# First pair's loads split over two queues, its bounds over three banks, its masks turned in two parts, and a new instruction order, in a chunk-selecting attention kernel on one core

## The chip, the core and the metric

The kernel runs on one core of one Trainium2 chip. The metric is the device time of one execution in microseconds (us); the median of the runs stands for a kernel. PE is the matrix engine (PEld its weight loads), DVE the vector engine, ACT the scalar engine, POOL the general one, SP the one that issues most DMAs. Each runs its instructions strictly in the order written, and waits on semaphores for the others.

## The reference

Attention over selected chunks of keys, then a gated linear unit with a causal convolution, in float32; four batches, eight heads, 768 positions, head size 64.

```python
k_chunks = k.reshape(B, H, nc, chunk, D)            # chunk = 32, nc = 24
k_min, k_max = np.min(k_chunks, axis=3), np.max(k_chunks, axis=3)
ub = np.sum(np.maximum(q[:, :, :, None, :] * k_min[:, :, None, :, :],
                       q[:, :, :, None, :] * k_max[:, :, None, :, :]), axis=-1)
ub = np.where(causal, ub, -1000000000.0)
top_chunks = np.argsort(ub, axis=-1)[..., -top_k:]  # top_k = 6
scores = scale * np.matmul(q, k.transpose(0, 1, 3, 2))
scores = np.where(mask, scores, -1000000000.0)      # selected chunk, and causal
attn = softmax(scores)
x = concatenate_heads(np.matmul(attn, v))           # (4, 768, 512)
gate = 1.0 / (1.0 + np.exp(-gate_pre))              # gate_pre: causal convolution of x, 5 taps
out = (gate * (x @ w_val)) @ w_out
```

## The kernel before

Two heads make a pair; there are 16 pairs (0 to 15), four to a batch, and each has six query tiles of 128 positions (0 to 5). A function `build` makes a graph of named operations, and `emit_in_order` writes them down in the order of a long table, `ORDER`. That table alone sets the order on each engine; `=7` behind a name is the PSUM bank (of eight) that the operation's group takes. A bank is free again when the last operation of its group has been written. No scheduler runs later.

The names, for pair p: `Lk`, `Lq`, `Lv` load keys, queries, values (for pair 0 keys and queries in two halves of 384 positions, `.0` and `.1`, each as two DMAs, one for each head, 96 KB apiece). `KT`, `QT` transpose them on PE (half `.0` or `.1`), `KE`, `QH` copy the result on ACT. `KX` reduces a half to the maximum or the minimum of each chunk on DVE. Only pair 0 computes its bounds in float32: `KF` copies the maxima (`.h0`) and the minima with the sign turned (`.h1`) of head h, `QF` and `RF` are the two parts of the queries by sign, on ACT, and `BF0.t` is the product for query tile t, one matmul with the causal fill and four passes of the float32 ones. (Later pairs do it with `QL`, `AH`, `AL` on DVE, `KB` on POOL and `CF`, `BD` on PE.) `T8` takes the eight largest bounds of a tile and head, `CM` compares with the sixth, which gives the mask `NS`. `MT` turns the masks of five tiles on PE, `ME` copies them to `QM` on DVE; `MD` does both as a DMA for pairs 10 to 15. `Sp.b` is a bank of scores (two matmul groups, one with the mask), `E` the exponential on ACT, `A` the causal cut on POOL, `AV` the product with the values (`VC` made them on POOL), `RC` and `NR` the division on DVE. `XT` turns the result, by DMA on SP for pairs 8 to 14, by PE and a copy `XTE` otherwise. `XH` copies the halo on POOL, `CV` is the convolution on PE, `TH` the gate on ACT, `VL` and `GV` the value product and the gating, `OU`, `OE`, `ST` the last product, its eviction and its store. `F0` to `F15` and `G0` to `G19` are filler matmuls on zeros that keep PE busy; `cwt` and `cws` turn the convolution's weights; `aw` is a small exponential that nothing reads.

Loads, stores and DMA transposes stand in one queue on SP, in the table's order. A DMA also waits until the one eight places earlier has landed, since eight semaphores are used in turn. Pair 0's five bound products share one bank, so `T8`, which waits for its bank, begins after the last of them.

## Time and profile before

| | us |
|---|---|
| runs of the kernel before (3) | 187.21 median, 186.26 to 188.31 |
| the profiled execution | 186.9 |
| its span in the profile | 185.2 |

A row of the timeline has start and length in us, engine, line of the code, operation, what it writes and reads, how many were merged, and in brackets the idle time before it with what ended it. A row of a stage table has the stretch and each engine's busy time in it. Busy time of PE counts matmuls from their start to their end, with their latency, so that PE can be busy and still have room. The granted clock was 1.00 throughout.

### The profile page before, as it was taken

The numbers are of one execution on the slowest core, as the hardware profiler recorded it, in microseconds if no ns is written. First come the engines' busy times: TensorE is split into PE (matmuls) and PEld (weight loads), VectorE is DVE, ScalarE is ACT, GpSimd is POOL, SyncE is SP. The second block draws the span as 40 slices with busy tenths as digits, with TensorE's granted clock in tenths as the row PEclk, the third lists the DMA queues.
The fourth block names the chain that finished last, engine by engine and source line by source line (L and its number), as shares of the span: only waits on it lengthen the run. The fifth ranks groups of instructions, "written<-read, shape, count | busy, mean of one in ns | idle before, by whom it ended". The sixth has DMA issues, their size and how long they took to land.

```text
span 185.2 us, 8893 instructions
## 1 busy us (share of the span) xinstructions
PE 176.5 (95%) x3714; PEld 127.2 (69%) x3714; DVE 125.8 (68%) x429; ACT 140.3 (76%) x320; POOL 109.6 (59%) x309
## 2 busy tenths in 40 slices
PE   7999999999999999989899999998999999999992
PEld 5696666878876787767667685786667677656441
DVE  0569999989999889998664579558923432710370
ACT  2369999999999799998698767595765979248032
POOL 7965899999999958899729423248641634100000
PEclk9999999999999999999999999999999999999999
DMA  5999989999999999960679993895047239537046
GB/s 106 213 221 217 204 189 231 193 192 229 195 210 190 211 217 199 226 122 4 144 133 178 183 209 98 178 98 151 4 81 90 69 95 173 153 119 282 8 173 224
DMA packets 89912, 29.68 MB, mean 160 GB/s; under 512 B 85387, under 2 KB 86667, under 8 KB 89872
## 3 DMA queue, kind: packets, MB, share of 16 engines
q1 hardware_dynamic: 88880, 28.06, 73.0%
q0 software_dynamic: 992, 1.06, 4.1%
q8 instruction: 29, 0.48, 1.1%
q14 instruction: 11, 0.09, 0.2%
HBM read 20.98 MB, written 6.29 MB: 147 GB/s over the span
## 4 chain that ended last, share of the span: by engine, by line
PE 59%; DVE 23%; DMA 7%; issue 3%; POOL 2%; ACT 2%; SPq 2%; DVEq 0%; POOLq 0%; ACTq 0%
PE ps L917 10%; PE ps L931 9%; DVE KK L653 8%; PE ps L902 7%; PE ps L838 7%; PE ps L810 6%; PE ps L640 6%; PE ps L813 5%; DMA vn<-in_v_dram 3%; PE ps L765 3%; DVE ON L848 3%; DVE TOP L773 3%; DMA xT<-ON 3%; DVE QL L721 2%; DVE RH L728 2%
## 5 line engine op out<-in xcount | busy, mean ns | idle before, releaser
L817 ACT ACTIVATE P<-ps 128x512 f16<-128x512 f32 (+1 forms) x192 | 89.6, 596 | 7.1 <-PE ps L813 6.6
L829 POOL TENSOR_SCALAR_AFFINE_SELECT P<-P 128x256 f16<-128x256 f16 (+1 forms) x128 | 43.6, 363 | 19.7 <-ACT P L817 18.2
L813 PE MATMUL ps<-QM,EM 64*128 64x512 f16 (+4 forms) x256 | 37.4, 290 | 0.3
L653 DVE TENSOR_REDUCE KK<-ps 128x12 f32<-128x384 f32 x64 | 32.8, 549 | 6.8 <-PE ps L640 6.4
L810 PE MATMUL ps<-QH,KE 64*128 64x512 f16 (+4 forms) x256 | 35.7, 291 | 0.0
L923 DVE SCALAR_TENSOR_TENSOR GV<-G,ps 128x384 f16<-128x384 f32 x32 | 16.3, 549 | 23.6 <-PE ps L917 23.6
L838 PE MATMUL ps<-VA,P 128*128 128x65 f16 x672 | 30.7, 194 | 0.9 <-DVE KK L653 0.6
L838 PEld LDWEIGHTS <-P 128*128 128x128 f16 x672 | 26.3, 98 | 6.5 <-issue 2.9
L917 PE MATMUL ps<-xT,wv 64*128 64x384 f16 x256 | 24.1, 323 | 0.5 <-issue 0.5
L939 ACT ACTIVATE OSB<-ps 128x512 f32<-128x512 f32 (+1 forms) x22 | 12.9, 597 | 15.0 <-PE ps L931 7.7
L931 PE MATMUL ps<-wo,GV 128*128 128x512 f16 (+1 forms) x100 | 22.9, 370 | 0.0
L773 DVE MAX8 TOP<-ps 128x8 f32<-128x16 f32 (+4 forms) x160 | 15.9, 166 | 8.3 <-PE ps L765 5.4
L907 ACT ACTIVATE G<-ps 128x384 f32<-128x384 f32 x32 | 14.0, 502 | 8.4 <-PE ps L902 8.3
L740 POOL CAST VA<-vn 128x768 f16<-128x768 f32 x16 | 14.3, 892 | 9.2 <-DMA vn<-in_v_dram 9.1
L917 PEld LDWEIGHTS <-wv 64*128 64x128 f16 x256 | 13.5, 94 | 8.8 <-issue 1.9
L647 ACT ACTIVATE KE<-ps 128x384 f16<-128x384 f32 x32 | 16.8, 564 | 2.3 <-DVE KK L653 1.5
L810 PEld LDWEIGHTS <-KE 64*128 64x128 f16 x256 | 14.0, 94 | 6.1 <-issue 1.6
L902 PE MATMUL ps<-xT,diag 32*32 32x384 f16 x1280 | 17.5, 326 | 0.6 <-issue 0.5
L848 DVE TENSOR_TENSOR ON<-ps,RCP 128x384 f16<-128x384 f32 x32 | 17.5, 553 | 0.7
L682 ACT ACTIVATE QH<-ps 128x384 f16<-128x384 f32 x32 | 15.7, 543 | 3.0 <-PE ps L640 3.0
L902 PEld LDWEIGHTS <-diag 32*32 32x32 f16 x1280 | 14.2, 88 | 3.4 <-issue 1.7
L640 PE MATMUL ps<-ident,kn 128*128 128x128 f32 x96 | 15.5, 281 | 0.3 <-DMA kn<-in_k_dram 0.3
(75 smaller groups left out, 305.7 us busy)
## 6 DMA issues: line engine op xcount, KB each, us to landing
vn<-in_v_dram SPq DMA_DIRECT2D x16, 384.0 KB, 6.3
out_dram<-OSB SPq DMA_DIRECT2D x23, 256.0 KB, 2.8
kn<-in_k_dram SPq DMA_DIRECT2D x30, 192.0 KB, 4.8
qn<-in_q_dram SPq DMA_DIRECT2D x30, 192.0 KB, 5.2
wv<-in_moe_w_val_dram POOLq DMA_DIRECT2D x8, 64.0 KB, 4.4
wo<-in_moe_w_out_dram POOLq DMA_DIRECT2D x4, 128.0 KB, 4.8
wv<-wv SPq DMA_DIRECT2D x4, 128.0 KB, 4.7
qn<-in_q_dram SPq DMA_DIRECT2D x4, 96.0 KB, 2.8
```

The source lines that it names most:

```text
L640: nc.tensor.transpose(out=pt[:, tl * 128:(tl + 1) * 128], in_=t[:, 3 * w + tl, :], identity=ident)
L653: nc.vector.tensor_reduce(out=KK[p % 2][:, mx, w * 12:(w + 1) * 12], in_=bank(gr, None).rearrange("p (c t) -> p c t", t=CH), axis=AX.X, op ...
L773: nc.vector.max(out=TOP[p % 2][:, it - 1, s, :], in_=bounds(gr)[:, it - 1, s * NCH:s * NCH + n])
L810: nc.tensor.matmul(out=pq[hh][:, col + a:col + n], lhsT=KE[p % 3][HP[hh], ks], rhs=QH[p % 3][HP[hh], q0 + a:q0 + n], start=True, stop=False)
L813: nc.tensor.matmul(out=pq[hh][:, col + a:col + n], lhsT=EM[HP[hh], ks], rhs=qm[HP[hh], q0 + a - 128:q0 + n - 128], start=False, stop=True)
L817: e.EX = lambda p, hh, bi, tot, gr: nc.scalar.activation(out=PT[hh, bi, p % 2][:, 0:tot], in_=bank(gr, None)[:, 0:tot], func=AF.Exp, scale ...
L829: nc.gpsimd.affine_select(out=ap, in_=ap, pattern=[[0, n], [1, 128]], compare_op=ALU.is_ge, fill=0.0, base=0, channel_multiplier=-1)
L838: nc.tensor.matmul(out=pav[:, qt, :], lhsT=PT[a, bi, p % 2][:, col:col + 128], rhs=VA[p % 3][:, hh, jt, :], start=(jt == 0), stop=(jt == qt))
L848: e.NR = lambda p, hh, gr: nc.vector.tensor_tensor(out=ON[(p // 2) % 2][:, 2 * (p % 2) + hh].rearrange("p t h d -> p h t d"), in0=bank(gr, ...
L902: nc.tensor.matmul(out=pc[i][os], lhsT=diag[rs, cp * NG + gi, j, :], rhs=x[rs, gi, :, a:a + 128], start=(j == 0), stop=(j == 2 * KSZ - 1), ...
L917: nc.tensor.matmul(out=pv[h], lhsT=wval_sb[HP[h], n, wc:wc + 255:2], rhs=xT[HP[h], (b % 2) * 2 + cp, gi, :, LD:LD + 128], start=(n == 0), ...
L931: nc.tensor.matmul(out=po[:, 0:z - a], lhsT=GVT[(b % 2) * NCT + et][:, s * 128:(s + 1) * 128], rhs=wout_sb[:, et, a:z], start=(et == 0), s ...
```

## The change

For pair 0, head 0's four loads of keys and queries stay on SP, and head 1's four are issued by ACT. The bounds of tiles 5 and 4, of 3 and 2, and of 1 take a bank each. The negated minima (`KF`) move from ACT to DVE. The masks are turned as tiles 2 to 5 (`MT0`, `ME0`) and as tile 1 (`MU0`, `MV0`), and only the score banks that hold tile 1 wait for the second part. The whole table is new: 110 lines replace as many; one of each is shown.

```diff
 ORDER = """
-mKF0 wval30 mfz F0=0 F1 F2 F3 F4 F5 mxT F6 F7 F8 ident identb mKB1 cfill identh mVA0 F9 F10 F11 F12
...
+mNS0 mfz Hq0.1 F0=0 F1 mKF0 F2 F3 F4 Hq0.0 Hk0.0 cwl F5 F6 F7 F8 F9 F10 F11 F12 F13 F14 F15 G12=1
...
+BGRP = {5: 0, 4: 0, 3: 1, 2: 1, 1: 2}
...
             for part in range(nsp):
                 ks = [(key, k4, 0), (key, k4, 1)] if nsp == 1 else [(key, k4, part)]
+                if nsp == 2:
+                    for hh, en in enumerate(("SP", "ACT")):
+                        g.op(en, 500, 500, "LH"[hh] + f"{what}{p}.{part}",
+                             lambda part=part, hh=hh, en=en: e.load(what, p, part, nsp, en, (hh,)), (),
+                             [(key, k4, part, "h")[:3 + hh]], dma=1800.0 / 4)
+                    continue
...
-                    g.op("ACT", 90, 205, f"KF{p}.{hh}{n}", lambda hh=hh, n=n: e.KFb(p, hh, n), kks,
+                    eng = "DVE" if n else "ACT"
+                    g.op(eng, 90, 205, f"KF{p}.{hh}{n}", lambda hh=hh, n=n: e.KFb(p, hh, n), kks,
                          [("KF", k2, hh, n)], ())
...
-        gr = g.group()
+        gs = [g.group() for _ in range(3 if full else 1)]
+        bg = {it: gs[BGRP[it] if full else 0] for it in range(1, NT)}
         for it in range(1, NT):
+            gr = bg[it]
...
-            gr = g.group()
-            g.op("PE", 5 * 56, 4 * 56 + 225, f"MT{p}", lambda gr=gr: e.MT(p, gr),
-                 nsk + [("identh",)], [("mps", p)], [gr])
...
+            for x, a, z, ks in (("T", 2, NT, 0), ("U", 1, 2, 1)) if full else (("T", 1, NT, None),):
+                gr = g.group()
+                qk = qmk if ks is None else [qmk[ks]]
+                g.op("PE", (z - a) * 56, (z - a - 1) * 56 + 225, f"M{x}{p}",
+                     lambda a=a, z=z, gr=gr: e.MT(p, gr, a, z),
+                     [("NS", k2, it) for it in range(a, z)] + [("identh",)], [("mps", p, a)], [gr])
...
-                 + [("QM", k3), ("EM",)],
+                 + qmk[:1 + (bi in (1, 3))] + [("EM",)],
...
     def KFb(p, hh, n):
-        nc.scalar.activation(out=KF[HP[hh], n, CC[hh] * NCH:(CC[hh] + 1) * NCH],
-                             in_=KK[p % 2][HP[hh], n], func=AF.Copy, scale=-1.0 if n else 1.0)
+        o, i = KF[HP[hh], n, CC[hh] * NCH:(CC[hh] + 1) * NCH], KK[p % 2][HP[hh], n]
+        if n:
+            nc.vector.tensor_scalar(out=o, in0=i, scalar1=-1.0, scalar2=None, op0=ALU.mult)
+        else:
+            nc.scalar.activation(out=o, in_=i, func=AF.Copy)
```

In the new table the filler stands partly behind the first scores (`G7`, `G9`, `G18`, `G1`, `G4`, `G6`, `G16`; before only `G8`), as do `cwt` and `cws`; `aw` stands near the end.

What the table does to the order of the engines, at three places. Numbers are buffers: `kn_74` and `qn_78` hold pair 0's keys and queries, `kn_75` and `qn_79` pair 1's, `qn_80` pair 2's. First the start of SP, before:

```order
L1092 UNCONDITIONAL_BRANCH
L631 DMA qn_78<-in_q_dram 128x3x64 x2
L631 DMA kn_74<-in_k_dram 128x3x64 x4
L631 DMA kn_75<-in_k_dram 128x6x64 x2
L631 DMA qn_78<-in_q_dram 128x3x64 x2
L631 DMA qn_80<-in_q_dram 128x6x64 x2
```

Now the start of SP:

```order
L1110 UNCONDITIONAL_BRANCH
L646 DMA kn_74<-in_k_dram 128x3x64 x2
L646 DMA qn_78<-in_q_dram 128x3x64
L646 DMA kn_75<-in_k_dram 128x6x64 x2
L646 DMA qn_78<-in_q_dram 128x3x64
L646 DMA qn_80<-in_q_dram 128x6x64 x2
```

And the start of ACT now, which before began with the table load:

```order
L1110 UNCONDITIONAL_BRANCH
L646 DMA qn_78<-in_q_dram 128x3x64 x2
L646 DMA kn_74<-in_k_dram 128x3x64 x2
L718 ACT_TABLE_LOAD
L718 ACTIVATE QF<-ps_224 128x256
```

Four of the pair's eight loads have gone from SP to ACT, ahead of its table load; ACT's last is the second half of the keys. Second, DVE from pair 0's reductions to its masks, before:

```order
L653 TENSOR_REDUCE KK_107<-ps_221 128x12 x2
L653 TENSOR_REDUCE KK_107<-ps_234 128x12 x2
L999 TENSOR_REDUCE ident_63<-identh 128x32
L653 TENSOR_REDUCE KK_108<-ps_261 128x12 x2
L653 TENSOR_REDUCE KK_108<-ps_267 128x12 x2
L773 MAX TOP_117<-ps_284 128x8 x10
L780 TENSOR_TENSOR NS_119<-ps_284,TOP_117 128x2x24 x5
```

Now the same stretch of DVE (`KK_108` are pair 1's reductions, `QM` the turned masks):

```order
L668 TENSOR_REDUCE KK_108<-ps_252 128x12 x2
L668 TENSOR_REDUCE KK_108<-ps_263 128x12
L791 MAX TOP_117<-ps_278 128x8 x2
L791 MAX TOP_117<-ps_291 128x8 x2
L798 TENSOR_TENSOR NS_119<-ps_278,TOP_117 128x2x24
L668 TENSOR_REDUCE KK_108<-ps_263 128x12
L791 MAX TOP_117<-ps_285 128x8 x4
L798 TENSOR_TENSOR NS_119<-ps_285,TOP_117 128x2x24 x2
L791 MAX TOP_117<-ps_291 128x8 x2
L798 TENSOR_TENSOR NS_119<-ps_291,TOP_117 128x2x24 x2
L812 COPY QM_89<-ps_332 128x128
```

The ten `MAX` have become four groups from three banks, one reduction of pair 1 stands between them, and the masks are copied in two pieces. Third, SP near the end, before (`xT<-ON` are `XT12`, `XT13` and `XT14`):

```order
L944 DMA out_dram<-OSB_167 128x512
L862 DMA_TRANSPOSE xT<-ON_149 128x6x128
L944 DMA out_dram<-OSB_174 128x512
L944 DMA out_dram<-OSB_168 128x512
L862 DMA_TRANSPOSE xT<-ON_149 128x6x128
L944 DMA out_dram<-OSB_171 128x512
L944 DMA out_dram<-OSB_172 128x512
L862 DMA_TRANSPOSE xT<-ON_150 128x6x128
```

The same place now (`vn_85` are pair 15's values, the first store is `ST1.5`):

```order
L962 DMA out_dram<-OSB_170 128x512
L962 DMA out_dram<-OSB_167 128x512
L962 DMA out_dram<-OSB_172 128x512
L880 DMA_TRANSPOSE xT<-ON_149 128x6x128
L642 DMA vn_85<-in_v_dram 128x12x64
L880 DMA_TRANSPOSE xT<-ON_149 128x6x128
L962 DMA out_dram<-OSB_173 128x512
L962 DMA out_dram<-OSB_174 128x512
L880 DMA_TRANSPOSE xT<-ON_150 128x6x128
```

A load of 384 KB that stood some twenty DMAs earlier has come between the two transposes `XT12` and `XT13`.

## The prediction

> **What bounds the kernel now.** I read the head of the page first, then a table of the stages, then the first 15.5 us instruction by instruction, and last the DMA queue towards the end. The head of the page (time and span, PE's own line, and what the DMA engines moved in 40 slices of 4.63 us):

> ```profile
> span 185.2 us, 8893 instructions
> PE 176.5 (95%) x3714; PEld 127.2 (69%) x3714; DVE 125.8 (68%) x429; ACT 140.3 (76%) x320; POOL 109.6 (59%) x309
> GB/s 106 213 221 217 204 189 231 193 192 229 195 210 190 211 217 199 226 122 4 144 133 178 183 209 98 178 98 151 4 81 90 69 95 173 153 119 282 8 173 224
> ```

> The table of stages has, for each stretch, its length, then busy us (instructions) of PE, PEld, DVE, ACT and POOL, the granted clock, the DMA share and GB/s:

> ```profile
> 0.00:15.50 15.50, 13.88 (x114) 10.95 (x115) 7.58 (x33) 7.75 (x20) 11.91 (x33) 1.00 1.06 185
> 15.50:60.00 44.50, 43.73 (x786) 32.58 (x786) 42.90 (x162) 44.12 (x105) 39.42 (x109) 1.00 1.06 204
> 60.00:100.00 40.00, 38.42 (x1065) 29.59 (x1065) 34.28 (x110) 35.09 (x81) 30.97 (x86) 1.00 0.80 155
> 100.00:140.00 40.00, 39.21 (x744) 27.53 (x753) 25.54 (x91) 28.65 (x64) 19.51 (x59) 1.00 0.66 128
> 140.00:175.00 35.00, 34.74 (x1001) 23.49 (x971) 11.13 (x30) 21.92 (x49) 7.78 (x24) 1.00 0.52 131
> 175.00:185.20 10.20, 6.53 (x37) 3.03 (x32) 4.42 (x9) 2.77 (x5) 0.00 (x0) 1.00 0.48 180
> ```

> The 95% of PE hides three regimes. Up to 15.5 us PE is busy with filler and transposes while DVE and ACT work half the time: the first pair's chain sets the pace. From 15.5 to 60 us ACT (44.12 of 44.50) and DVE (42.90) are both full. After 100 us ACT and DVE fall off and PE alone is full. So a shorter start moves the ACT-bound stretch forward as a whole, and is kept at the end if nothing later takes it back.

> **The start, before.** Columns: start, length, engine, line, operation.

> ```profile
> 0.80 0.98 SPq L631 DMA_DIRECT2D qn<-in_q_dram  x2
> 1.83 3.52 SPq L631 DMA_DIRECT2D kn<-in_k_dram  x6
> 5.44 0.52 PE L640 MATMUL ps<-ident,kn 128*128 128x128 f32 x3
> 6.67 0.52 PE L640 MATMUL ps<-ident,kn 128*128 128x128 f32 x3 [0.27 <-DMA kn<-in_k_dram]
> 7.22 1.02 DVE L653 TENSOR_REDUCE KK<-ps 128x12 f32<-128x384 f32 x2 [0.21 <-PE ps L640]
> 8.16 0.35 DVE L999 TENSOR_REDUCE ident<-identh 128x32 f16<-128x128 f16 x1
> 8.99 1.95 DVE L653 TENSOR_REDUCE KK<-ps 128x12 f32<-128x384 f32 x4 [0.48 <-PE ps L640]
> 9.02 0.33 ACT L688 ACTIVATE KF<-KK 64x24 f32<-64x24 f32 x2
> 9.79 0.19 PE L705 MATMUL ps<-cfill,identb 128*128 128x48 bf16 x1
> 11.77 0.62 PE L713 MATMUL ps<-KF,QF 128*128 128x48 f32 x4
> 9.88 0.87 ACT L700 ACTIVATE QF<-ps 128x384 f32<-128x384 f32 x2 [0.15 <-PE ps L640]
> 12.43 0.91 DVE L773 MAX8 TOP<-ps 128x8 f32<-128x24 f32 x10 [1.49 <-PE ps L713]
> 13.29 0.67 DVE L780 TENSOR_TENSOR NS<-ps,TOP 128x48 f16<-128x48 f32 x5
> 14.50 0.49 DVE L794 COPY QM<-ps 128x640 f16<-128x640 f16 x1
> 15.49 1.09 ACT L817 ACTIVATE P<-ps 128x512 f16<-128x512 f32 x2 [0.16 <-PE ps L813]
> ```

> Read downwards: the second half of the keys is what PE waits for (6.67); its maxima and minima end at 8.24, the last KF copy at 9.35, five bound products run 9.79 to 12.39 (0.49 each), and only then DVE starts its ten MAX8, because all five share one bank (1.49 idle). Masks end at 13.96, their turned copy at 14.99, the first exponential starts at 15.49.

> **The change, step by step.** *Loads.* The eight 96 KB loads of pair 0 go four to SP and four to ACT. How long one takes to land:

> ```profile
> qn<-in_q_dram SPq DMA_DIRECT2D x4, 96.0 KB, 2.8
> kn<-in_k_dram SPq DMA_DIRECT2D x4, 96.0 KB, 3.1
> 0.79 1.28 ACT L700 ACT_TABLE_LOAD   x1 [0.79 <-PEq L1081]
> ```

> SP needs some 0.52 us an issue (six in 3.52, waits included, or two in 0.98). No row shows ACT issuing; at SP's price its four take 2.1 us, the table load follows, and ACT is free at 4.2, before the first transposed keys. KT0.1 now comes first and needs the fourth ACT load. Lower bound: issued at 0.80 + 3 x 0.52 = 2.36, landed 3.1 later, at 5.46, transposed at 5.6. Upper bound, by the bytes: the first load lands at 0.80 + 2.8 = 3.6 and seven more follow at 96 KB by 213 GB/s, 0.46 each: 6.8, transposed at 6.95. The load issued at 2.35 before was transposed at 5.44 and the sixth at 6.67, so I take 6.05, below the middle.

> *From there.* Reductions 0.55 later as before: 6.60 to 7.6, the small one (0.35) to 7.9, the other two to 8.85. Two KF copies on DVE, two on ACT (0.33): 9.2. PE also has QT0.1 ahead of the bounds, waiting for SP's last load of the pair, which waits until one of the first has landed (3.6) and is twelfth in bytes with pair 1's keys ahead: it lands between 3.6 + 0.5 + 2.8 = 6.9 and 3.6 + 11 x 0.46 = 8.7, in time. Then DVE has three reductions of pair 1 (0.49 each) to 10.6 while ACT makes QF0.1 and RF0.1 (0.87) to 10.1, so the product BF0.5 runs 10.2 to 10.85. MAX8 of tile 5 (0.18) and one mask (0.2) end at 11.2; the displaced reduction at 11.7; tiles 3 and 2 at 12.3; tile 4, whose product ends at 12.2 behind a transposition, at 12.8. Four transposes to 13.25 (five, with the wakes around them, took 13.96 to 14.50), meanwhile the one-tile copy (0.2) and a QL on DVE (0.4, an estimate: 256 columns against a reduction's 384); the four-tile copy (0.4, five tiles took 0.49) ends at 13.75. From there to the exponential 0.50, as before (14.99 to 15.49): 14.25. **Gain 1.2**; with the bounds of the loads 0.3 to 1.6. Three banks instead of one bring what DVE does between 10.6 and 12.4; the price is that DVE, not PE, now paces the end.

> *What it adds.* One more DVE copy (0.2) and two KF copies moved from ACT (0.25): DVE is 1.6 below full from 15.5 to 60, so 0 to 0.4, and I take 0, since they lie in the start counted above. Moved behind the first scores: six more fillers and the eight small transposes of cwt.

> ```profile
> 7.02 1.36 PE L949 MATMUL ps<-fz 128*128 128x256 f16 x11
> 13.00 0.65 PE L1039 MATMUL ps<-ident,cwn 5*128 5x5 f32 x8
> ```

> That is 6 x 0.12 + 0.6 = 1.3 us more PE work after the first score. It lies beside the full ACT; if that cover is missing it costs up to 1.3.

> *The end.* The tiny `aw` moves between the last TH (0.2 at most, ACT has room). The last stores swap halves: two issues back to back, 0 to 0.4, take 0.1. On SP, XT12, Lv15 and XT13 now stand in a row behind ST1.5, ST0.0 and ST0.5, ahead of CV13:

> ```profile
> 118.17 4.51 SPq L862 DMA_TRANSPOSE xT<-ON  x1
> 150.01 2.01 SPq L862 DMA_TRANSPOSE xT<-ON  x1
> 152.07 1.04 SPq L944 DMA_DIRECT2D out_dram<-OSB  x2
> 153.22 2.41 SPq L862 DMA_TRANSPOSE xT<-ON  x1
> 158.18 0.46 POOL L889 COPY xT<-xT 128x32 f16<-128x32 f16 x2 [0.25 <-DMA xT<-ON]
> L627 SPq DMA_DIRECT2D vn<-in_v_dram x16: 483/998/2994, 17.6 to 117.3; - x16
> 156.15 2.67 PE L838 MATMUL ps<-VA,P 128*128 128x65 f16 x78
> 162.74 2.06 PE L902 MATMUL ps<-xT,diag 32*32 32x384 f16 x160
> 164.72 2.76 PE L931 MATMUL ps<-wo,GV 128*128 128x512 f16 x12
> 151.96 0.22 PE ps L813 x2
> 152.18 1.30 PE ps L917 x16
> ```

> From the end of OU1.5: its eviction and wakes 0.8, store 0.35, two stores 1.04, XT12 2.01, the v load 0.48 to 2.99, XT13 to landing 4.96 (153.22 to 158.18; 7.1 if its issue takes the 4.51 of the one that stood behind two v loads), XH13 0.46: 10.1 to 14.8. PE's cover: 28 AV matmuls at 0.034, CV9 2.0 (162.74 to 164.72), S15 about 2.2 (an estimate: 10 times 512 columns of two heads at 0.22), three VL of 1.30, one OU 0.92: 9.9. The last two rows are of the chain of waits. So a stall of 0.2 to 4.9; I take 0.2, by the medians.

> *Sum.* -1.2 + 0.1 + 0.2 = -0.9, and for everything else that the new order permutes, 0. The profiled execution took 186.9, 1.7 around its span, and would come to 186.0; the median of the runs shown, 187.21, to **186.3**.

> **Rivals.** *The rest of the order is better too.* From 15.5 to 175 us PE is idle 0.77 + 1.58 + 0.79 + 0.26 = 3.4; half of that filled is 1.7: 184.6. For it: in 60 to 100 us no engine is full. Against: nothing but a search says it.

> *The loads come no earlier.* DMA moved 213 GB/s in the second slice, close to its level while saturated, so more issue may only lengthen landing. At the upper bound, 6.95, the start gains 0.3: 187.2. [...]

> *PE gives it back.* If PE, not ACT, limits from 15.5 to 60, the 1.3 us of moved work cancel the gain: 187.6. For: 43.73 of 44.50. Against: a busy PE includes its latency, and ACT is fuller.

> *Slower: CV13 waits for XT13.* By the chain above; PE executes in order, so all behind CV13 waits with it. It decides once the chain exceeds cover by 3: the v load near 3 us and XT13's issue near 4.5. Loss 4.9: 191.0. Against: at 118 us two v loads stood ahead, here one.

> **The numbers.** Likeliest case 0.47 (its own range 185.3 to 187.3), better order 0.2, no earlier loads 0.1, given back 0.1, XT13 0.13. A measurement of this kernel tells about 1% from no change, that is 185.34 and 189.08. Faster by over 1%: the better order and a little of the likeliest, 0.26. Slower: XT13 and 0.01 besides, 0.14. Within: 0.60. Range 184.3 to 189.0: it leaves out the far part of the better order (about 0.06) and most of XT13.

> **What would show it.** The first exponential at 14.0 to 15.2, not 15.49; its ten MAX8 in four groups; ACT above 43 of the 44.5 us behind it; KT0.1 at 5.6 to 7.0; no PE gap above 0.5 us ahead of CV13. I am wrong if the first exponential comes 1 us earlier and the end does not, or if the time between start and end changes by more than 1 us: then the permuted order, for which I took 0, is the larger term.

## The result, and the profile after

| | before | after |
|---|---|---|
| median of 4 runs each, on one chip, us | 186.84 (186.26 to 188.31) | 188.88 (188.61 to 189.93) |
| ratio, with its 95% interval | | 1.0146 (1.0104 to 1.0189) |
| the profiled execution, its span, us | 186.9, 185.2 | 188.92, 187.2 |

The changed kernel is 1.5% slower, by more than a measurement can miss. The time lies inside the range given, and on the other side of no change than the forecast. (Comparisons leave disturbed runs out, so a ratio can differ a little from that of two medians.) The head of the page, for the kernel after; PEclk is the granted clock in tenths, in 40 slices:

```profile
span 187.2 us, 8913 instructions
PE 176.6 (94%) x3714; PEld 127.1 (68%) x3714; DVE 123.6 (66%) x432; ACT 139.3 (74%) x318; POOL 109.2 (58%) x309
PEclk9879999999999999999987999999999999999998
GB/s 138 219 217 219 192 230 197 191 231 176 216 189 226 200 170 190 14 18 99 203 123 159 208 67 77 234 30 162 54 172 106 59 208 80 116 148 231 180 172 220
```

PE has the same 3714 matmuls and the same busy time as before. What is new is the clock: before, it read 1.00 throughout; now it dips in the second and third slice and once in the middle (0.50 from 97 to 100 us, behind a wait of PE of 1.80 us that comes up again under "Fewer fillers"). The stages show where (columns as before):

```profile
0.00:15.50 15.50, 12.15 (x81) 10.04 (x82) 6.24 (x28) 5.45 (x14) 8.95 (x26) 0.89 1.15 194
15.50:60.00 44.50, 43.96 (x792) 33.20 (x790) 42.43 (x158) 44.41 (x107) 37.11 (x108) 1.00 1.02 206
60.00:100.00 40.00, 38.01 (x977) 28.89 (x978) 31.57 (x118) 36.21 (x83) 33.20 (x87) 0.96 0.67 127
140.00:175.00 35.00, 34.19 (x935) 22.49 (x917) 10.64 (x25) 22.49 (x50) 9.80 (x30) 1.00 0.61 148
```

ACT is full from 15.5 to 60 as before (44.41 of 44.50). The start is not shorter but emptier: PE 12.15 us busy instead of 13.88, with 81 matmuls instead of 114. The chain of waits of the first 20 us, followed back from what ended last, says why. Columns: start, length, and the work or the wait it lies in.

```profile
1.90 0.51 ACTq L646
2.44 4.53 DMA kn<-in_k_dram
6.97 0.14 issue
7.11 1.20 PE ps L655 x9
8.31 2.56 PE ps L967 x12
10.87 1.37 PE ps L655 x9
12.27 0.47 PE ps L731 x4
```

A load of keys that ACT issued at 2.44 lands at 6.97. From there on every link is PE, in the order written: the transposes of pair 0 (L655), twelve fillers (L967), more transposes, and only at 12.1 the first bound (L731), which before stood at 9.8. The same place in the timeline:

```profile
1.12 3.76 PE L967 MATMUL ps<-fz 128*128 128x256 f16 x17 [1.12 <-DVE fz L980]
2.37 1.70 SPq L646 DMA_DIRECT2D kn<-in_k_dram  x2
7.11 0.85 PE L655 MATMUL ps<-ident,kn 128*128 128x128 f32 x6 [2.23 <-DMA kn<-in_k_dram]
8.12 2.75 PE L967 MATMUL ps<-fz 128*128 128x256 f16 x12
9.93 0.36 DVE L705 TENSOR_SCALAR KF<-KK 64x24 f32<-64x24 f32 x2
11.31 0.61 PE L655 MATMUL ps<-ident,qn 128*128 128x128 f32 x3
12.08 0.19 PE L723 MATMUL ps<-cfill,identb 128*128 128x48 bf16 x1
12.96 0.24 DVE L791 MAX8 TOP<-ps 128x8 f32<-128x8 f32 x2
16.94 1.48 ACT L835 ACTIVATE P<-ps 128x512 f16<-128x512 f32 x4
```

PE has nothing for 2.23 us and starts KT0.1 at 7.11 (6.67 before). Then the twelve fillers take 2.75 us, 0.23 each, where eleven took 1.36 before. The granted clock, by stretches of the same profile, explains that:

```profile
5.00:8.00 3.00, 0.89 (x8) 0.92 (x9) 0.33 (x1) 0.00 (x0) 2.87 (x8) 1.00 1.38 221
8.00:11.50 3.50, 3.50 (x19) 2.80 (x18) 2.24 (x7) 1.72 (x6) 1.19 (x2) 0.52 1.36 214
11.50:15.50 4.00, 4.00 (x41) 3.92 (x40) 3.39 (x19) 2.44 (x7) 0.65 (x4) 1.00 1.38 220
```

For 3.4 us behind the gap PE runs at half its clock. The minima (KF) were ready at 10.29, so the bounds, which begin with the causal fill (L723), then waited for PE's queue: fillers, KT1.0, QT0.1, KT1.1. The first exponential comes at 16.94 instead of 15.49. DMA moved 214 to 221 GB/s all that time.

The other place is CV13, as SP, PE and POOL show it:

```profile
149.66 1.26 SPq L880 DMA_TRANSPOSE xT<-ON  x1
151.03 1.29 SPq L642 DMA_DIRECT2D vn<-in_v_dram  x1
152.42 1.73 SPq L880 DMA_TRANSPOSE xT<-ON  x1
158.22 0.47 POOL L907 COPY xT<-xT 128x32 f16<-128x32 f16 x2 [3.63 <-DMA xT<-ON]
158.48 1.84 PE L920 MATMUL ps<-xT,diag 32*32 32x384 f16 x118 [0.81 <-POOL xT L907]
```

XT13, third in the row, needs 5.80 us from its issue to POOL's halo copy, and PE waits 0.81 us.

### The profile page after: what moved, and what is told of

The parts are those of the page before. It is cut to its first block, busy times and chain, and to the rows that moved or that the text cites. A ratio compares the mean times of both kernels' runs of the same rounds, so it can differ in the third digit from the quotient of the medians.

```text
span 187.2 us, 8913 instructions
## 1 busy us (share of the span) xinstructions
PE 176.6 (94%) x3714; PEld 127.1 (68%) x3714; DVE 123.6 (66%) x432; ACT 139.3 (74%) x318; POOL 109.2 (58%) x309
## 3 DMA queue, kind: packets, MB, share of 16 engines
q0 software_dynamic: 992, 1.06, 4.0%
## 4 chain that ended last, share of the span: by engine, by line
PE 83%; DMA 8%; ACT 4%; DVE 1%; issue 1%; ACTq 1%; SPq 0%; POOL 0%; POOLq 0%
PE ps L655 12%; PE ps L856 10%; PE ps L949 10%; PE ps L920 10%; PE ps L828 9%; PE ps L935 9%; PE ps L831 8%; PE ps L783 5%; DMA xT<-ON 5%; DMA kn<-in_k_dram 2%; ACT P L835 2%; PE ps L967 2%; PE ps L888 2%; PE ps L808 2%; PE ps L731 1%; PE ps L826 1%
## 5 line engine op out<-in xcount | busy, mean ns | idle before, releaser
L835 ACT ACTIVATE P<-ps 128x512 f16<-128x512 f32 (+1 forms) x192 | 91.7, 592 | 8.5 <-PE ps L831 8.2
L847 POOL TENSOR_SCALAR_AFFINE_SELECT P<-P 128x128 f16<-128x128 f16 (+1 forms) x128 | 43.7, 359 | 21.7 <-ACT P L835 20.5
L831 PE MATMUL ps<-QM,EM 64*128 64x512 f16 (+4 forms) x256 | 36.0, 290 | 0.0
L828 PE MATMUL ps<-QH,KE 64*128 64x512 f16 (+4 forms) x256 | 34.2, 291 | 1.8 <-ACT P L835 1.8
L856 PE MATMUL ps<-VA,P 128*128 128x65 f16 x672 | 29.6, 194 | 0.2 <-issue 0.2
L957 ACT ACTIVATE OSB<-ps 128x512 f32<-128x512 f32 (+1 forms) x22 | 12.8, 599 | 15.7 <-PE ps L949 13.2
L949 PE MATMUL ps<-wo,GV 128*128 128x512 f16 (+1 forms) x100 | 23.3, 370 | 0.0
L935 PE MATMUL ps<-xT,wv 64*128 64x384 f16 x256 | 23.0, 323 | 0.0
L791 DVE MAX8 TOP<-ps 128x8 f32<-128x8 f32 (+4 forms) x160 | 15.5, 164 | 7.4 <-PE ps L783 6.7
L655 PE MATMUL ps<-ident,kn 128*128 128x128 f32 x96 | 16.1, 290 | 2.3 <-DMA kn<-in_k_dram 2.2
L920 PEld LDWEIGHTS <-diag 32*32 32x32 f16 x1280 | 14.5, 88 | 5.0 <-issue 1.9
L678 POOL TENSOR_TENSOR KD<-KK 128x24 f32<-128x24 f32 x30 | 7.1, 246 | 18.3 <-DVE KK L668 13.1
L697 ACT ACTIVATE QH<-ps 128x384 f16<-128x384 f32 x32 | 16.8, 578 | 0.7 <-PE ps L655 0.7
L828 PEld LDWEIGHTS <-KE 64*128 64x128 f16 x256 | 12.8, 94 | 6.0 <-issue 0.9
```

Of the source, the lines that this page charges most:

```text
L655: nc.tensor.transpose(out=pt[:, tl * 128:(tl + 1) * 128], in_=t[:, 3 * w + tl, :], identity=ident)
L828: nc.tensor.matmul(out=pq[hh][:, col + a:col + n], lhsT=KE[p % 3][HP[hh], ks], rhs=QH[p % 3][HP[hh], q0 + a:q0 + n], start=True, stop=False)
L831: nc.tensor.matmul(out=pq[hh][:, col + a:col + n], lhsT=EM[HP[hh], ks], rhs=qm[HP[hh], q0 + a - 128:q0 + n - 128], start=False, stop=True)
L835: e.EX = lambda p, hh, bi, tot, gr: nc.scalar.activation(out=PT[hh, bi, p % 2][:, 0:tot], in_=bank(gr, None)[:, 0:tot], func=AF.Exp, scale ...
L847: nc.gpsimd.affine_select(out=ap, in_=ap, pattern=[[0, n], [1, 128]], compare_op=ALU.is_ge, fill=0.0, base=0, channel_multiplier=-1)
L856: nc.tensor.matmul(out=pav[:, qt, :], lhsT=PT[a, bi, p % 2][:, col:col + 128], rhs=VA[p % 3][:, hh, jt, :], start=(jt == 0), stop=(jt == qt))
```

## The experiments

Two theories stood at first. A: the loss is the late start. B: it arises behind CV11, since the changed kernel is 0.64 us ahead of before there (138.91 against 139.55, starts of CV11) and 1.92 behind at PE's end.

**Mixed tables.** Four kernels joined the two tables at one point: the start of one and the rest of the other.

x1_old_start, the seam at pair 1's first score:

```diff
 KB2.3 KT3.0=1 KE3.0 Lk4.0
-S1.5=60 E1.05 E1.15 A0.04 KE3.1 A0.11 dg01
+wval20 A0.15 A0.04 KX3.11 KE3.1 S1.1=64 E1.11 Lv0 KX3.00
```

> The kernel before up to the first score of pair 1 (21.6 us), then everything in the changed table's order; pair 0's loads, bank and masks as before. Theory A (the loss is the late start, first score 1.5 us late, and nothing behind it costs): 186.8, as the kernel before. Theory B (the loss arises behind CV11, where the changed kernel is 0.6 ahead in its profile and 2.0 behind at the end): 187.4, the changed kernel less the 1.5 of the start. Theory C (the order in the middle is better, the start and the end are worse): also 187.4, with CV11 ahead of before by some 2.

Measured: 195.38 us, ratio 1.0404 (1.0329 to 1.048). Neither theory. A row of the waits, PE from 20 to 40 us (engine and line waiting, what it waited for, us in total, times, longest):

```profile
PE ps L808 <- DVE ON L848: 2.3, 1, 2.3
```

With three more waits of 1.0 to 1.2 us it makes the seam itself dearer than what was to be measured. What late transfer or operation stands behind them was not followed up.

x2_new_start, the other way round:

```diff
 MT1=7 ME1 cwt=3 cws G6 G16
-S1.1=20 E1.11 A0.05 A0.03 Lv0 Lk4.0
+wval30 mxT mVA1 wval21 A0.05 dg03 A0.03 Lq3.0 QT3.1=5 QH3.1 QT3.0=2 Lk4.0
+S1.5=47 E1.05 E1.15 A0.11 dg01
```

> The changed kernel up to the first score of pair 1 (split loads, three banks, masks in two parts, its order), then the order of the kernel before. Theory A (all of the loss is the start): 188.9 at most, 188.3 if the 1.5 us come through whole. Theory B: the start is absorbed before the end, as the changed kernel's own 1.5 was by CV11: 186.8 to 187.3.

Measured: 189.88 us, 1.0148 (1.0091 to 1.0206). In its profile the first exponential is at 16.83, 1.34 us later than before, and PE ends 1.97 us later than before. The late start is not absorbed, so that part of B is gone. It does not show A alone: CV1 starts at 63.48, 2.97 later than before, so this seam costs something too.

x3_old_to_CV11 and x4_new_to_CV11, the seam at CV11:

```diff
 T815.1 XT11 XH11
-CV11.0=0342 CV11.1 TH11.01 TH11.11 TH11.00 S14.5=15
+A13.03 A13.05 T815.4 NR12.1 S14.0=30 E14.10 E14.00 T815.5 CM15
+CV11.0=7043 CV11.1 TH11.10 TH11.01 TH11.00 S14.5=21
```

> The kernel before up to the convolution CV11 (139.5 us), then the changed table's order, with XT12, the load of pair 15's values and XT13 in a row ahead of CV13 (that load stood earlier and stays earlier here, since it was already issued: only the two transposes stand in a row). Theory A: 186.8, since the start is that of before. Theory B (the end of the changed table costs 2.6 whatever is ahead of it): 189.4. Theory B' (in that end it is the load between the two transposes): 187 to 187.6.

> The changed kernel up to CV11 (138.9 us, 0.6 ahead of before in the profiles), then the order of before. Theory A: 188.3 to 188.9, late as the changed kernel. Theory B: 186.2, before less 0.6, so faster than both.

Measured: 190.2 us, 1.0179 (1.0126 to 1.0231), and 188.56 us, 1.0094 (1.0048 to 1.014). Both are slow, but in x3 CV11 itself had come 2.8 us later than before and in x4 2.3 later than in the changed kernel, since the operations that only one table has ahead of CV11 were pulled in front of it. So they decide nothing on B. Edits inside the changed table serve better.

**The order of the loads.**

```diff
-mNS0 mfz Hq0.1 F0=0 F1 mKF0 F2 F3 F4 Hq0.0 Hk0.0 cwl
+mNS0 mfz Hk0.1 Hk0.0 Hq0.0 Hq0.1 Lk0.1 Lk0.0 Lq0.0 Lq0.1 F0=0 F1 mKF0 F2 F3 F4 cwl
...
-Lk0.0 Hk0.1 ident Lk0.1 KT0.1=2
+ident KT0.1=2
```

> The changed kernel, with one thing altered: pair 0's eight loads are issued with the halves KT0.1 and KT0.0 need first (keys .1, keys .0, queries .0, queries .1 on each queue), all ahead of pair 1's keys. Theory A (the start is late because the second half of the keys is the last of the bytes in flight, 7.11 us for KT0.1, and PE's 2.2 us without work then halve the granted clock for 3.4 us): KT0.1 at 4.9 to 5.6, no stretch of clock below 0.9 before 15 us, first exponential at 14.5 to 15.0 instead of 16.94, and the end follows by 1.3 to 2.2: 186.7 to 187.6. Rival (the loads come no earlier whatever their order, since all share the same engines): KT0.1 at 7, 188.9. Rival (the start comes earlier but the middle is set by something else, loads or the order): first exponential earlier by 2, end 188.5 to 189.

Measured: 186.23 us, 1.002 (0.9981 to 1.0059): nearly the whole loss is gone. With the same bytes, queues and engines, only the order in which they are asked for is another. So A stands, and the rival that the loads come no earlier whatever their order falls.

**Fillers ahead of the gap.**

```diff
-Lk0.1 KT0.1=2 em0 identh
+Lk0.1 G2 G13 G17 G10 G19 G11 G14 G3 G15 G8 G0 G5 KT0.1=2 em0 identh
```

> The changed kernel with twelve of its fillers (G) moved from behind the first transposes to ahead of KT0.1, where PE had 2.2 us without work. Loads and all else as there. Theory A' (the halved clock and the fillers in the way are the larger part of the late start): KT0.1 still at 7.1, but granted clock at 1.00 throughout the start, bounds from 10.4 instead of 12.1, first exponential at 15.2 to 15.7, the end 1 to 1.5 earlier: 187.4 to 187.9. Rival (only the loads matter): first exponential within 0.4 of 16.9, 188.5 to 189.

Measured: 187.36 us, 1.0059 (1.0011 to 1.0108), 1.5 less than the changed kernel, as A' said. The keys still come at 7.2:

```profile
7.22 0.85 PE L655 MATMUL ps<-ident,kn 128*128 128x128 f32 x6 [0.30 <-DMA kn<-in_k_dram]
8.23 0.49 PE L655 MATMUL ps<-ident,kn 128*128 128x128 f32 x3
10.22 0.66 PE L731 MATMUL ps<-KF,QF 128*128 128x48 f32 x4 [0.76 <-ACT KF L707]
```

And a stretch of it:

```profile
11.50:15.50 4.00, 4.00 (x31) 3.68 (x30) 3.16 (x21) 2.86 (x7) 2.24 (x8) 0.69 1.39 219
```

The first bound is 1.9 us earlier. The clock was not mended in the execution that was profiled (189.53 us): its half-speed stretch comes later (0.69 from 11.5 to 15.5), and the first exponential at 16.64, outside the expectation. By the mean clock listed with each run, six of the twelve had none (1.00; 185.35 to 187.56 us) and a seventh hardly any (0.997; 185.26); all four of the changed kernel had at least one (0.977 and 0.991: 3.4 us at half speed are 1.7 of 187, or 0.009).

**The load between the transposes.**

```diff
-AV13.00=1 ST0.4 Lv14 XH9 OU1.1=5
+AV13.00=1 ST0.4 Lv14 Lv15 XH9 OU1.1=5
...
-ST0.0 ST0.5 XT12 Lv15 XT13 VC14 XH13
+ST0.0 ST0.5 XT12 XT13 VC14 XH13
```

> The changed kernel with the load of pair 15's values issued right behind that of pair 14, instead of between XT12 and XT13. Theory T (the wait ahead of CV13, 0.8 us in the changed kernel, is that load ahead of XT13): XT13 lands 1.3 or more earlier, PE has no idle time ahead of CV13, 188.1. Rival (PE's work behind takes up the wait, or XT13 was late for OU1.5 and its store): 188.9.

Measured: 187.89 us, 1.0099 (1.0059 to 1.0139). The two transposes, the halo copy and CV13 in its profile:

```profile
149.34 3.11 SPq L880 DMA_TRANSPOSE xT<-ON  x2
154.40 0.46 POOL L907 COPY xT<-xT 128x32 f16<-128x32 f16 x2 [0.20 <-DMA xT<-ON]
157.25 2.06 PE L920 MATMUL ps<-xT,diag 32*32 32x384 f16 x160
```

The halo copy comes 3.8 us earlier, PE waits for nothing, and the time is 0.99 lower. The intervals of the two ratios overlap, but the same edit on top of k1 (c1, below) has them apart, and from CV11's start to PE's end v1 is 0.97 us shorter than the changed kernel, and c1 than k1 by as much. Theory T holds, and B in this one place.

**Bounds ahead of everything of pair 1.**

```diff
-KF0.11 KF0.01 KT1.0=5 KX1.01 KX1.00 Lq0.1 QT0.1=6 KT1.1=7 KX1.10
+KF0.11 KF0.01 QT0.1=6 KF0.00 KF0.10 BF0.1=0 T80.1 QF0.1 BF0.2=4 RF0.1
...
+KT1.0=5 MU0=6 MV0 KT1.1=7 MT0=4 ME0 S0.2=63 E0.02 KX1.01 KX1.00 S0.5=04
```

> As the run with the keys first, and besides pair 0's second half of queries, its bounds, masks and first score stand ahead of pair 1's turned keys and their reductions on PE, DVE and ACT. Theory A: bounds from 8.3, masks by 11.5, first exponential at 12.0 to 13.0, so 3.9 to 4.9 earlier than in the changed kernel; carried to the end by half or more: 184.3 to 186.5. Rival (what is won at the start is lost behind it, because pair 1's reductions come later or the loads are the limit from 15 to 30 us): 187 to 189.

Measured: 189.33 us, 1.0185 (1.0125 to 1.0245), which is the rival's time. But nothing was won at the start either: the first exponential of its profile is at 14.77, that of k1 at 14.55. Stretches of it:

```profile
10.00:12.00 2.00, 1.58 (x11) 1.58 (x11) 0.84 (x6) 0.00 (x0) 0.00 (x0) 0.73 1.32 208
12.00:14.00 2.00, 2.00 (x14) 1.58 (x13) 0.85 (x6) 0.00 (x0) 0.00 (x0) 0.50 1.38 220
16.00:18.00 2.00, 1.37 (x12) 1.36 (x13) 0.42 (x2) 1.74 (x6) 1.44 (x6) 1.00 1.38 217
```

With pair 1's transposes out of the way PE has gaps again, the clock halves from about 11 to 14, and behind the first scores PE waits for what DVE and ACT now do late for pair 1.

**Both mendings together.** The edits of k1 and v1.

> The changed kernel with both mendings: pair 0's keys first on both queues, and pair 15's values loaded right behind pair 14's. If the late keys and the load between the transposes are two separate losses (2.65 us and 1.0 us by the medians of those two runs), 185.2 to 185.6, ratio to the kernel before 0.993 to 0.999. Rival (the second loss was only there because the first had pushed the work; or PE's later work takes it up): 186.2, as with the keys first alone.

Measured: 184.45 us, 0.9906 (0.9868 to 0.9944), below the expectation and faster than both kernels. Its start:

```profile
4.72 1.30 PE L655 MATMUL ps<-ident,kn 128*128 128x128 f32 x6
6.18 1.47 PE L967 MATMUL ps<-fz 128*128 128x256 f16 x12
8.41 0.52 PE L655 MATMUL ps<-ident,kn 128*128 128x128 f32 x3 [0.75 <-DMA kn<-in_k_dram]
9.42 0.19 PE L723 MATMUL ps<-cfill,identb 128*128 128x48 bf16 x1
10.37 0.24 DVE L791 MAX8 TOP<-ps 128x8 f32<-128x8 f32 x2
14.28 1.48 ACT L835 ACTIVATE P<-ps 128x512 f16<-128x512 f32 x4
```

Keys are turned at 4.72, right behind the fillers; twelve fillers take 1.47 us at full clock; the first exponential is 2.66 us earlier than in the changed kernel. Why the two edits together earn 0.75 more than the lower end of the expectation was not traced; k1 lists a mean clock of 0.991 or less in seven of its twelve runs, c1 in two of eight, which may be part of it. The starts of some operations in the three profiles, by the order of each table:

| us | before | after | c1 |
|---|---|---|---|
| first score | 14.73 | 16.28 | 13.62 |
| CV1 | 60.51 | 61.85 | 59.20 |
| pair 8's first score | 73.90 | 75.30 | 72.34 |
| CV11 | 139.55 | 138.91 | 135.94 |
| PE's last end | 181.53 | 183.45 | 179.34 |

**One queue instead of two.**

```diff
-for hh, en in enumerate(("SP", "ACT")):
+for hh, en in enumerate(("SP", "SP")):
...
-Hk0.1 Hk0.0 Hq0.0 Hq0.1 Lk0.1 Lk0.0 Lq0.0 Lq0.1
+Lk0.1 Hk0.1 Lk0.0 Hk0.0 Lq0.0 Hq0.0 Lq0.1 Hq0.1
```

> The kernel with the keys first, but all eight loads of pair 0 issued by SP, one behind the other (keys .1 of both heads, keys .0, queries .0, queries .1), none by ACT. Theory Q (the two issuers share the same DMA engines, so the order of the bytes counts and the number of queues does not): KT0.1 within 0.4 us of the 4.8 there, first exponential within 0.5, time within 0.5 of 186.2. Rival (the second issuer's 2 us of earlier issue is what makes the start): pair 1's keys and the second half of the queries 1 to 2 us later, first exponential 1 us later, 187.0 to 187.5.

Measured: 186.39 us, 0.9998 (0.9967 to 1.0028); k1 with two queues had 1.002 (0.9981 to 1.0059). No difference in time. KT0.1 stands at 4.72 here too; pair 1's keys come later (9.32 instead of 8.41 in c1) and the first exponential at 15.19, 0.64 behind k1's 14.55 and 0.91 behind c1's 14.28, so nearer to the rival's 1 us than within theory Q's 0.5. What earned is the order, not the second queue; that what was lost at the start did not reach the end is measured, and its way was not traced.

**The split alone, in the kernel before.**

```diff
-F13 Lq0.0 F14 F15 G14=1 G12 G13 G10 G11 G9 Lk0.0 KT0.0=2
+F13 F14 F15 G14=1 G12 G13 G10 G11 G9 KT0.0=2
...
+Hk0.0 Hk0.1 Hq0.0 Hq0.1 Lk0.0 Lk0.1 Lq0.0 Lq0.1 F0=0
```

> The kernel before with one part of the change alone: pair 0's eight loads on two queues, keys ahead of queries (.0 ahead of .1 as its transposes stand), all ahead of pair 1's. One bank, masks in one part, table otherwise as before. Theory (the split is worth what it moves the second half of the keys): KT0.0 at 5.4 as before, since fillers end there, KT0.1 at 5.8 instead of 6.67, first exponential 0.5 to 0.9 earlier, 185.9 to 186.5 beside 186.8 for before. Rival (nothing, since the bounds wait for something else): within 0.2 of before.

Measured: 186.38 us, 1.0005 (0.9972 to 1.0038): the rival. In its profile KT0.0 starts at 5.89 and KT0.1 at 7.28, behind QT0.0 and a filler in PE's queue, and the first exponential at 15.95. This profile cannot price the split: in it the first fillers, 22 as before, take 4.87 us instead of 4.29, so PE itself came to KT0.0 later (more on that under "The clock").

**Fewer fillers.** The edits of c1, and G7, G9, G18, G1, G4, G6, G16 left out.

> As the run with both mendings, with seven of the fillers (those that stand behind the first score; zeros into a spare bank) left out. Two theories of PE's wait of 1.0 to 1.8 us at 91 to 95 us, at the second matmul of S10.2, which the changed order has in every run and before does not: if it belongs to that operation (its bank, its reader), it stays at that matmul; if it belongs to a count of instructions (their supply to PE), it comes 14 instructions later, in the bounds of pair 11 or S10.0. The time: 0 to 0.8 less, since the fillers are 7 x 0.11 of PE's work beside a full ACT.

Measured: 185.03 us, 0.9917 (0.9877 to 0.9957), the same as c1. The wait of PE, first in the changed kernel, with ACT beside it, then in this one:

```profile
91.54 3.05 ACT L835 ACTIVATE P<-ps 128x512 f16<-128x512 f32 x6
95.55 0.37 PE L828 MATMUL ps<-QH,KE 64*128 64x512 f16 x1 [1.80 <-ACT P L835]
```

```profile
93.60 0.20 PE L783 MATMUL ps<-KB,QH 128*128 128x48 f16 x1 [1.41 <-issue]
```

In the first the profile names ACT, but ACT had been done since 94.59, nearly 1 us. In the second the wait has moved on, past the scores, to a bound product (L783), and nothing is named. The matmul that waits is the 1742nd of the trace in both kernels: the wait keeps the count, not the operation.

**Banks, masks, first bound.** Three edits of c1, each alone.

```diff
-BGRP = {5: 0, 4: 0, 3: 1, 2: 1, 1: 2}
+BGRP = {5: 0, 4: 0, 3: 0, 2: 0, 1: 0}
...
-BF0.1=0 T80.1 QF0.1 BF0.2=4 RF0.1 KE1.0 BF0.5=2 T80.5
+BF0.1=0 QF0.1 BF0.2 RF0.1 KE1.0 BF0.5 QH0.1 KX1.11 BF0.3 Lq2.0 QT2.0=5 BF0.4 T80.1 T80.5
```

> The run with both mendings, with pair 0's bounds back in one PSUM bank: its ten MAX8 and five masks stand behind the last of the five products on DVE. Theory (the three banks are the part of the change that earns at the start): the masks' copies end 1.0 to 1.2 us later, first exponential at 15.2 to 15.5 instead of 14.28, and the end follows: 185.2 to 185.8. Rival (DVE's pair 1 reductions fill the time until then and the rest is absorbed): 184.2 to 184.7.

Measured: 187.9 us, 1.0037 (0.9994 to 1.0079), against 0.9906 for c1, so some 1.3%, 2.4 us, and more than the theory's 1.2. The first exponential of its profile is at 17.92. PE waits for DVE's masks, and behind that the clock is at 0.50:

```profile
12.78 0.91 DVE L791 MAX8 TOP<-ps 128x8 f32<-128x8 f32 x10 [1.50 <-PE ps L731]
13.86 0.23 PE L808 MATMUL ps<-identh,NS 128*128 128x128 f16 x1 [1.11 <-DVE NS L798]
```

```profile
16.00:17.00 1.00, 1.00 (x8) 0.65 (x8) 0.68 (x2) 0.42 (x2) 0.00 (x0) 0.50 1.40 226
```

```diff
-for x, a, z, ks in (("T", 2, NT, 0), ("U", 1, 2, 1)) if full else (("T", 1, NT, None),):
+for x, a, z, ks in (("T", 1, NT, None),):
```

> The run with both mendings, with pair 0's masks turned and copied in one part as before. Theory (the two parts are worth a tenth or two at the start): first exponential 0 to 0.3 later, 184.4 to 184.8. Rival (the scores without tile 1 start much earlier by the split): first exponential 0.5 or more later, 185 or more.

Measured: 184.46 us, 0.9935 (0.9898 to 0.9971), first exponential at 14.45: the two parts are worth 0.2 at the start and nothing that shows at the end.

```diff
-KT1.0=5 KX1.01 KX1.00 QT0.1=6 KT1.1=7 KX1.10 KF0.00 KF0.10 BF0.1=0 T80.1
+QT0.1=6 KF0.00 KF0.10 BF0.1=0 KT1.0=5 T80.1 KX1.01 KX1.00 KT1.1=7 KX1.10
```

> The run with both mendings, with pair 0's second half of queries and its first bound ahead of pair 1's turned keys on PE, where PE waited 0.75 us for those keys. Theory (the queue on PE still costs the start): first bound at 8.8 instead of 9.5, first exponential at 13.6 to 14.1, 183.8 to 184.4. Rival (DVE paces the start, or pair 1's reductions come later by as much): first exponential within 0.2 of 14.28, 184.3 to 185.

Measured: 184.18 us, 0.9929 (0.989 to 0.9968). The first bound (its L731) is at 8.67 instead of 9.45 and the first MAX8 1 us earlier, yet the first exponential at 14.33: the rival, DVE paces this start.

## Why the prediction was wrong, step by step

- **Loads: the step that failed.** "I take 6.05", between bounds of 5.6 and 6.95; it was 7.11. The upper bound counted the eight loads of pair 0 alone. But SP issued pair 1's keys, two times 192 KB, from 2.37 on, while the last load that KT0.1 needs left ACT at 2.44. The profile counts both queues against the same 16 engines (up to 9 us SP's took 77.0% of their time and ACT's 22.1%); together they moved 221 GB/s from 5 to 8 us, and that load needed 4.53 us. k1 shows the cause: asked for first, the same keys are turned at 4.54.
- **From there: also failed, with a cost the prediction has no term for.** Even by its own 6.05 PE, done with its fillers at 4.9, would have stood idle for a microsecond; I priced only what came later, not the gap. Behind the gap the clock was halved for 3.4 us (0.52 from 8.0 to 11.5), and twelve fillers and three groups of transposes ahead of the bounds took until 12.1. QT0.1's load was in time, as forecast (in f1, with the same loads, PE turns it at 8.56), but behind the fillers it ran only at 11.31. f1, with its fillers ahead of the gap, puts the gap and the fillers behind it at 1.5 us.
- **"DVE, not PE, now paces the end"** was wrong in the changed kernel, where the chain is PE from 7.11 on, and right once the keys come early (k3).
- **The gain of 1.2 at the start** seems to come in c1, 14.28 for the first exponential beside 14.25 forecast, but that agreement is luck. Its keys are turned 1.3 earlier than I took (4.72, not 6.05), and from there to the first bound it needs 4.70 us, where before needs 3.12 (6.67 to 9.79) and I counted about 3.2 (6.05 to the last `KF` at 9.2): twelve fillers and pair 1's keys stand in between. What held is the second half. From the first bound to the first exponential it takes 4.86 us in the changed kernel, in k1, in c1 and in s1, and 5.70 before, so the new order of bounds and masks is worth 0.84 there, even in the slower kernel. m1 shows that it needs the three banks (8.13 with one, half clock included); the masks in two parts are worth 0.1 to 0.2 of it (m2), and two queues nothing that these runs can tell in time (s1, b1). The three banks in the order of before were not tried.
- **Moved fillers and copies, taken 0:** right for the fillers (c2: 0.9917 beside 0.9906); the copies and the small transposes were not tried alone.
- **The end, taken 0.2 within 0.2 to 4.9:** a stall of 0.81 was there, worth 0.99 of the time (v1). The mis-sized term is XT13's landing: 5.80 us to the halo copy where I put 4.96, the load beside it being in flight. Cover was as counted: from OU1.5's end at 147.58 to 157.67, 10.1 beside 9.9.
- **The rest of the order, taken 0:** it is not 0. By the table of starts c1 gains 2.5 us on before between the first score and CV11 (1.1 ahead, then 3.6) and gives back 1.4 behind it; whether its end is worse or only has more left to do there is open. That gain is the rival "the rest of the order is better too", whose 184.6 is close to the 184.45 of c1, a kernel with two more edits, so the nearness is partly luck. The profile of the changed kernel is ahead of before at CV11 as well, in spite of PE's wait of 1.80 us and the half clock behind it.
- **The other rivals.** "The loads come no earlier" was right in its premise and wrong in its price, 187.2, since it reckoned only with the keys. What a second issuer is worth was not shown before the change; s1 and k1 show it: with SP alone DMA moved 108 GB/s up to 5 us and 216 from 5 to 8, with SP and ACT 145 and 224, and the times are 186.39 and 186.23 us. "Slower: CV13 waits" was real, at a fifth of its 4.9. "PE gives it back" did not happen.
- **What would show it:** MAX8 in four groups and ACT above 43 came; the first exponential at 14.0 to 15.2, KT0.1 by 7.0 and no gap above 0.5 ahead of CV13 did not.

In sum the forecast was -1.2 for the start and +0.3 for the end. The first exponential came 1.45 later; the middle made up 2.1 by CV11; and 2.6 went again behind it, 1.1 by the load between the transposes (the difference to c1 grows by that) and the 1.4 that c1 loses too.

## What to carry to other kernels

Where a start waits for loads, count all bytes in flight up to the one that is needed, those of later work too, and ask for the needed ones first (188.88 us became 186.23 in k1); a second issuing engine did not replace that here (188.88 with two and the keys late, 186.39 with one and the keys first). Where PE has to wait, look at what it has between its last filler and the first arrival: a gap of 1 to 2 us can cost twice, itself and the half clock behind it (there was one behind 1.11, 1.80 and 2.23 us, and none behind 1.25), and fillers behind the gap stand in the way of what it waited for. A table that sets the order is tuned as a whole: join two, and the seam can cost more than what was to be measured; edits of a few names tell more.

## What the runs showed of the hardware that was not expected

The listed clock does not show all of it. x2 has the start of the changed kernel, and its clock is listed as 1.00 from end to end. Yet behind the gap its matmuls run at half pace until about 10.2:

```profile
7.17 1.51 PE L655 MATMUL ps<-ident,kn 128*128 128x128 f32 x6 [2.25 <-DMA kn<-in_k_dram]
9.11 2.05 PE L967 MATMUL ps<-fz 128*128 128x256 f16 x12
```

The same six take 0.85 us in the changed kernel, the same twelve 1.47 in c1. The first fillers of a kernel are slow too at a listed 1.00: 17 take 3.76 us in the changed kernel, 0.22 each. Between the profiles the end of that first slow stretch lies anywhere from about 4.1 (m1) to 7.1 us (b1), and starts compared to a few tenths contain this. The length of matmuls of one shape tells PE's pace where the listed clock does not.

**The supply of PE's instructions.** Unexplained waits of PE of 0.4 to 1.8 us fall on one count. Counting PE's records in the trace (weight loads, matmuls, semaphore instructions), the wait of 1.80 us in the changed kernel stands ahead of the 3522nd, at the second matmul of S10.2, and k1 (1.53 us), f1 (1.81), v1 (0.99), x4 (1.32) and c1 (0.42) wait at the same matmul. Before has a wait of 0.50 ahead of the 3266th, 256 earlier, and c2 (1.41, seven matmuls further on, with seven fillers fewer ahead of it) shows that the count decides. The queue that brings instructions has this line on the page of the kernel after (packets, MB, share of the engines):

```profile
q8 instruction: 29, 0.48, 1.1%
```

That is 16 KB a packet. They begin where PE stands at 218 to 7386 of its 7484 records, on average 256 apart. In the changed kernel one ran from 92.46 to 94.14, and PE went on at 95.55, while DMA moved 208 to 220 GB/s (92 to 95 us). So this wait looks like PE running dry of instructions while loads fill the DMA engines; that it belongs to the count is shown, that the packet is late for the loads is only the author's estimate. If it is such a packet, one of the 29 cost 1.80 us in the changed kernel.
